# Eight-batch attention feeding a gated expert layer on one core: load order, staged keys for the second batch, and column halves of the second weight

## The chip, the cores and the metric

The kernel runs on one core of a Trainium2 chip. The metric is the time of one execution on the device in microseconds (us). The kernel before took 373.83 us as the median of three runs (373.21 to 375.34). One more execution was taken by the hardware profiler: it took 373.17 us, of which 371.5 us lie between its first and its last instruction (the span).

## The reference: what is computed

There are T = 8 batches of S = 576 tokens, H = 8 heads, D = 64 numbers per head. First comes attention with a bias that depends on the distance of two tokens alone:

```
scores = q @ k.T / sqrt(64) + bias[head, bucket(|i - j|)]     # per batch and head
x      = softmax(scores) @ v                                  # [4608 tokens, 512]
h      = x @ w_in                                             # [4608, 2048]
g      = h + sin(alpha * h) ** 2 / alpha
out    = g @ w_out                                            # [4608, 512], float32
```

All inputs are float32 in the device's memory. The kernel computes in 16-bit floats with sums in float32. Beyond a distance of 128 the bias is constant, so the kernel takes the constant out of the softmax and multiplies the exponentials by a table of ratios (the band, `m2`) only near the diagonal.

## The kernel before, in words

**Tiling.** The heads go in four pairs, so that two heads of 64 numbers fill 128 partitions. Of the 576 keys of a batch, four chunks of 128 are "A" units and the last 64 are "C" units (tile `kt`, in which a pair's two heads stand on the diagonal of a 128 x 128 block with zeros beside them). The last 64 queries are "B" and "X" units; for batch 0 they are put off into batch 1. A unit is a score matmul (TensorE, line 601), an exponential (ScalarE, line 887, 1024 columns at a time) and a product with the band (VectorE, lines 919, 932, 897; for C units line 905, on GpSimd or VectorE). Then the attention matmuls with the values follow, and after a division (lines 1137 and 1138) the result is turned into the token buffer `xT`, by TensorE (line 1209) or by a transposing DMA (line 1200). In `mh` stand copies of those parts of the band that the C and X units need (line 763); they are made from `m2` in two halves, one for each 64 partitions.

**The expert layer** works on nine blocks of 512 tokens. For each of 16 slices `f` of the 2048 middle columns there are four matmuls of 512 columns, a sine (line 1253), a square (1260 or 1262) and a sum (1267) that gives `g[f]`. The sums of TensorE stand in eight banks: six for scores and for the middle columns, two (6 and 7) for attention and for the output. `plan_mo` makes the output: for each 128 tokens 16 matmuls of 512 columns, a copy (lines 672 or 674) and a DMA. These output matmuls are the filler: TensorE does them when nothing else is ready. `xT` is a ring of 1728 tokens (three batches). A block of 512 that crosses its end, as blocks 3 and 6 do, is computed with two matmuls in place of each one.

**The order of the work** is made when the kernel is built. `Plan.run` walks through a list of tasks with estimated durations and puts each on the engine on which it can start first; the priorities only break ties within 0.02 us. `HEAD_PRI` holds priorities for tasks by their number in the list. While scores are computed, fillers are counted: at most 32 matmuls in batch 1 (`QUOTA1`), 44 in the later ones, spread evenly; past that number a filler is taken only where TensorE would else stand idle for over 0.2 us (`FILL_GAP`). What comes out is one fixed order for each engine, with semaphores between them.

**The head.** Keys and queries come from memory with a token per row and must be turned, so that the 64 numbers of a head lie along partitions. For batch 0 and batch 1, `load_nat` (line 576) loads them as they are and TensorE turns them (`plan_tr`, line 691: 12 small matmuls for a pair's keys or queries), after which ScalarE or VectorE copies them to `kT` and `qT`, and GpSimd or VectorE copies the last 64 keys into `kt` (line 716). From batch 2 on, GpSimd's DMA queue copies keys and queries, cast to 16 bits, into a buffer in the device's memory (`stage`, line 532), and SyncE's queue brings them in with a transposing DMA (lines 542 and 545). The loads on GpSimd's queue have one order, that of `plan_loads`: pairs 1 and 2 of batch 0 (`STATIC`), batch 0's values and then pair 3's keys and queries (`LOADS`), `w_in` in three parts, batch 1's keys and queries, `w_out` in four parts of four `f` each, batch 1's values, and the staging of batch 2.

Of the kernel before, what the change touches and what calls it, by code (L numbers as in the profile page):

```python
# [13 lines left out]
ALU = mybir.AluOpType  # L14
# [47 lines left out]
class Plan:  # L62
# [165 lines left out]
LOADS = ((0, (0,)), (0, (1,)), (0, (2,)), (0, (3,)), (0, (4,)), (0, (5,)), (1, (3, 0)), (1, (3, 1)))  # L228
STAGED = ()
N_WO = 4  # L230
# [186 lines left out]
def kernel(  # L417
# [21 lines left out]
    SI = 6  # L439
# [987 lines left out]
```

## Time and profile before

| what | value |
|---|---|
| median of three runs | 373.83 us (373.21 to 375.34) |
| profiled execution | 373.17 us, span 371.5 us |
| TensorE matmuls, busy | 364.9 us (98% of the span), 3661 instructions |
| ScalarE, busy | 317.6 us (86%) |
| VectorE, busy | 263.1 us (71%) |
| GpSimd, busy | 88.5 us (24%) |
| granted TensorE clock | 1.0 throughout |

In the profile PE is TensorE's matmuls, PEld its weight loads, DVE is VectorE, ACT is ScalarE, POOL is GpSimd, SP is SyncE; the ending "q" stands for the DMA queue that an engine feeds. In a row of the order in time the first two numbers are start and duration in us, then engine, line, operation, what is written and read, the shape and the count; what stands in brackets is the idle time before it and what ended that. The ends of matmuls are modelled and overlap the next one's start, so the rate of a run of matmuls is read from the distance between the starts of two rows.

### The profile page before, as it was taken

The page shows a single profiled execution, that of the slowest core. Times are in us where ns is not written, and L with a number is a line of the kernel's source. Part 1 is how long each engine was busy: PE and PEld are TensorE (multiplying, and loading weights), DVE is VectorE, ACT ScalarE, POOL GpSimd, SP SyncE. Part 2 cuts the span into 40 slices and gives each one's busy share as a digit, 9 for nine tenths or more (in the row PEclk, how much of TensorE's full clock was granted, in tenths as well). Part 3 has the DMA queues.
Part 4 walks back from the last instruction along what each step waited for, and adds up shares of the span by engine and source line. Part 5 has one row for each costly group of instructions (what it writes and reads, how often), then busy time and mean ns, then how long its engine had stood idle before and what let it go on. Part 6 is the DMA issues. An engine that isn't in the chain of part 4 may idle for free.

```text
span 371.5 us, 9081 instructions
## 1 busy us (share of the span) xinstructions
PE 364.9 (98%) x3661; PEld 199.5 (54%) x3661; DVE 263.1 (71%) x575; ACT 317.6 (86%) x434; POOL 88.5 (24%) x115
## 2 busy tenths in 40 slices
PE   8989999999999999999999999999999999999996
PEld 5655445644464445784554456444666455444443
DVE  6897876777676967696759866887769675979100
ACT  3899999999997999899989999899989997999111
POOL 8764600064000900064004600290006000000000
PEclk9999999999999999999999999999999999999999
DMA  9999991799625992399829992699259121000112
GB/s 151 164 208 206 166 151 41 124 96 126 117 52 114 104 172 77 83 135 145 116 58 148 130 146 58 136 94 178 75 89 119 64 58 48 9 29 3 71 70 85
DMA packets 147993, 39.16 MB, mean 105 GB/s; under 512 B 136416, under 2 KB 142960, under 8 KB 147952
## 3 DMA queue, kind: packets, MB, share of 16 engines
q0 software_dynamic: 99664, 18.06, 60.9%
q1 hardware_dynamic: 47920, 20.11, 22.6%
q8 instruction: 28, 0.46, 0.5%
q10 hardware_dynamic: 368, 0.43, 0.4%
q14 instruction: 13, 0.11, 0.1%
HBM read 36.84 MB, written 16.52 MB: 144 GB/s over the span
## 4 chain that ended last, share of the span: by engine, by line
PE 95%; ACT 2%; DVE 2%; issue 0%; ACTq 0%
PE pb L601 92%; ACT u L887 2%; PE pb L691 1%; DVE u L919 1%; PE pb L1209 1%; PE pb L685 0%; DVE m L674 0%; DVE mh L763 0%; DVE qT L674 0%; DVE kT L674 0%; DVE kt L716 0%; DVE zz L639 0%; ACT outs L672 0%; DVE inv_a L831 0%; DVE alphaT L825 0%
## 5 line engine op out<-in xcount | busy, mean ns | idle before, releaser
L887 ACT ACTIVATE u<-pb 128x1024 f16<-128x1024 f32 (+1 forms) x146 | 137.1, 1018 | 9.9 <-PE pb L601 8.9
L601 PE MATMUL pb<-w_out,g 128*128 128x512 f16 (+2 forms) x592 | 140.0, 374 | 0.0
L601 PE MATMUL pb<-xT,w_in 128*128 128x512 f16 (+4 forms) x704 | 127.5, 340 | 0.0
L1267 DVE SCALAR_TENSOR_TENSOR g<-sq,inv_a,pb 128x512 f16<-128x512 f16 x144 | 101.0, 743 | 6.8 <-ACT sq L1260 3.3
L1253 ACT ACTIVATE s<-pb,alphaT 128x512 f16<-128x512 f32 x144 | 93.3, 690 | 11.9 <-PE pb L601 10.8
L601 PEld LDWEIGHTS <-w_in 128*128 128x128 f16 x704 | 64.6, 98 | 57.0
L601 PEld LDWEIGHTS <-g 128*128 128x128 f16 x592 | 53.5, 98 | 63.3 <-issue 9.7
L919 DVE TENSOR_TENSOR u<-u,m 128x768 f16<-128x768 f16 (+1 forms) x128 | 61.5, 489 | 30.2 <-ACT u L887 29.7
L601 PEld LDWEIGHTS <-u 128*128 128x128 f16 x1152 | 44.6, 97 | 9.4 <-issue 1.1
L554 POOL COPY kt<-kT 64x256 f16<-64x256 f16 x12 | 5.3, 445 | 178.2 <-PE pb L601 91.6
L601 PE MATMUL pb<-v,u 128*128 128x65 f16 x1024 | 44.0, 193 | 0.2
L601 PE MATMUL pb<-qT,kT 64*128 64x64 f16 (+1 forms) x512 | 42.1, 288 | 1.6 <-ACT u L887 1.4
L1260 ACT ACTIVATE sq<-s 128x512 f16<-128x512 f16 x69 | 42.8, 637 | 1.0 <-DVE g L1267 0.3
L1262 DVE TENSOR_TENSOR sq<-s 128x512 f16<-128x512 f16 x75 | 31.0, 425 | 13.8 <-ACT s L1253 13.0
L1138 DVE TENSOR_TENSOR xn<-pb,rd 128x256 f16<-128x256 f32 (+2 forms) x59 | 28.5, 483 | 2.0
L558 POOL DMA_DIRECT2D v<-in_v_dram x32 | 28.4, 898 | 1.1 <-DMA nat<-in_k_dram 0.8
L601 PE MATMUL pb<-vh,u 128*128 128x130 f16 x128 | 28.1, 219 | 0.0
L601 PEld LDWEIGHTS <-kT 64*128 64x128 f16 x512 | 16.3, 94 | 21.4 <-issue 14.3
L672 ACT ACTIVATE outs<-pb 128x512 f32<-128x512 f32 (+2 forms) x11 | 6.2, 568 | 20.4 <-PE pb L601 20.4
L1137 DVE RECIPROCAL rd<-pb 128x4 f32<-128x4 f32 (+2 forms) x59 | 11.0, 186 | 17.6 <-PE pb L601 17.5
L674 DVE COPY outs<-pb 128x512 f32<-128x512 f32 x26 | 17.9, 690 | 4.8 <-PE pb L601 4.6
L1332 ACT ACT_TABLE_LOAD x15 | 19.2, 1283 | 0.3
(72 smaller groups left out, 189.5 us busy)
## 6 DMA issues: line engine op xcount, KB each, us to landing
out_dram<-outs SPq DMA_DIRECT2D x35, 256.0 KB, 2.2
v<-in_v_dram POOLq DMA_DIRECT2D x32, 128.0 KB, 4.8
staged_k<-in_k_dram POOLq DMA_DIRECT2D x6, 576.0 KB, 8.9
staged_q<-in_q_dram POOLq DMA_DIRECT2D x6, 576.0 KB, 11.9
w_out<-in_moe_w_out_dram POOLq DMA_DIRECT2D x4, 512.0 KB, 18.2
w_in<-in_moe_w_in_dram POOLq DMA_DIRECT2D x2, 512.0 KB, 8.5
w_in<-in_moe_w_in_dram POOLq DMA_DIRECT2D x1, 1024.0 KB, 11.1
xT<-xn SPq DMA_TRANSPOSE x47, 2.4
```

Source lines behind the costliest of these rows:

```text
L558: nc.gpsimd.dma_start(out=vs[t % 2][:, c, :, 0:D], in_=vp[128 * c : 128 * c + 128],)
L601: nc.tensor.matmul(out=out, lhsT=lhsT, rhs=rhs, start=start, stop=stop)
L674: k_of(e).tensor_copy(out=o, in_=i)
L887: nc.scalar.activation(out=o, in_=x, func=AF.Exp, scale=0.125)
L919: nc.vector.tensor_tensor(out=io, in0=io, in1=m2[:, 2 * p : 2 * p + 2, x0 : x0 + hi - lo], op=ALU.mult)
L1137: nc.vector.reciprocal(out=r, in_=x[:, :, :, D])
L1138: nc.vector.tensor_tensor(out=xn[:, 0:n].rearrange("p c (z d) -> p c z d", z=2), in0=x[:, :, :, 0:D], in1=r.unsqueeze(3).to_broadcast([128 ...
L1253: nc.scalar.activation(out=s16.v, in_=h.v, func=AF.Sin, scale=alphaT[:, f : f + 1])
L1260: nc.scalar.activation(out=sq.v, in_=s16.v, func=AF.Square)
L1262: k_of(e).tensor_tensor(out=sq.v, in0=s16.v, in1=s16.v, op=ALU.mult)
L1267: nc.vector.scalar_tensor_tensor(out=gcell[b].v[:, f, :], in0=sq.v, scalar=inv_a[:, f : f + 1], in1=h.v, op0=ALU.mult, op1=ALU.add,)
L1332: nc.scalar.preload_act_table_set(name)
```

## The change

1. Pair 3's keys and queries of batch 0 move ahead of batch 0's values in GpSimd's load order.
2. Batch 1's keys are staged in the device's memory and turned by a DMA on SyncE's queue, as those of later batches are. Its queries are still turned by TensorE. The tile that took both is now half as large.
3. `w_out` is loaded in column halves (two parts of eight `f` for each half), the first half ahead of batch 1's values and the second behind them. Block 0's output is made in eight parts of 256 columns, the first two interleaved (12 `f` of the one, 12 of the other, then the remaining four of each).
4. `xT` is a ring of 2560 tokens (five blocks). No block of 512 crosses its end; the rows of batch 4 cross it, and are written in two pieces.
5. Batch 0's C units take the band directly from `m2`, with two products of 64 partitions each in place of one with `mh`. The two copies into `mh` get a late priority.
6. Some durations in the planner are new, and `HEAD_PRI` is another table.

```
-LOADS = ((0, (0,)), (0, (1,)), (0, (2,)), (0, (3,)), (0, (4,)), (0, (5,)), (1, (3, 0)), (1, (3, 1)))
-STAGED = ()
-N_WO = 4
+LOADS = ((1, (3, 0)), (1, (3, 1)), (0, (0,)), (0, (1,)), (0, (2,)), (0, (3,)), (0, (4,)), (0, (5,)))
+STAGED = (0,)
+N_WO = 2
...
-    XN = 3 * S
+    XN = 2560
...
-    def load_w_out16(fh):
+    def load_w_out16(c, fh):
         src = moe_w_out.rearrange("(f p) n -> p f n", p=128)
+        x = slice(c * DM // 2, (c + 1) * DM // 2)
         nc.gpsimd.dma_start(
-            out=w_out16[:, 4 * fh : 4 * fh + 4, :], in_=src[:, 4 * fh : 4 * fh + 4, :]
+            out=w_out16[:, 8 * fh : 8 * fh + 8, x], in_=src[:, 8 * fh : 8 * fh + 8, x]
         )
...
-            bands["h%d" % z] = plan.add({"POOL": 0.95, "DVE": 0.37}, half, [bands[0], bands[1]], -1000 + z)
+            bands["h%d" % z] = plan.add({"POOL": 0.95, "DVE": 0.37}, half, [bands[0], bands[1]], 10012 + z)
...
             def bd(e):
+                if t == 0:
+                    for z in range(2):
+                        r = slice(64 * z, 64 * z + 64)
+                        io = u.v[r, y, 8, 384:512]
+                        k_of(e).tensor_tensor(
+                            out=io, in0=io, in1=m2[r, 2 * p + z, 64 * z : 64 * z + 128], op=ALU.mult
+                        )
+                    return
...
-            d = plan.add({"POOL": 0.6} if t == 0 and p else {"DVE": 0.25 if two else 0.15}, bd, [x] + band,
+            d = plan.add({"DVE": 0.25} if t else {"POOL": 0.8, "DVE": 0.28}, bd, [x] + band,
                          base + 10, use=[ub])
...
-        x0 = S * t % XN + q0
+        x0 = (S * t + q0) % XN
         two = parts[-1][0] > p0
+        n0 = min(nq, (XN - x0) // 128)
+        cut = [(0, nq, x0)] if two or n0 == nq else [(0, n0, x0), (n0, nq, 0)]
...
-    def plan_mo(b, a):
+    def plan_mo(b, parts, cut=0):
 
-        for c0, c1 in ((0, 384), (384, DM)) if (b, a) == (T, 3) else ((0, DM),):
...
+        parts = [(a, c0, c1, Buf("mo"), Cell()) for a, c0, c1 in parts]
+        for f, (a, c0, c1, mb, m) in [(f, x) for lo, hi in ((0, cut), (cut, NF)) for x in parts for f in range(lo, hi)]:
...
-                        z = [plan.add({"DVE": 0.35}, lambda e: load_kt(1, nc.vector), y, 10080)]
+                        z = [plan.add({"POOL": 1.1, "DVE": 0.7}, lambda e: load_kt(1, k_of(e)), y, 10080)]
...
         for b in [t] if t < T - 1 else [t, t + 1]:
+            if b == 0:
+                n = DM // 2
+                plan_mo(b, [(0, 0, n), (1, 0, n)], 12)
+                for a, c0 in ((2, 0), (3, 0), (0, n), (1, n), (2, n), (3, n)):
+                    plan_mo(b, [(a, c0, c0 + n)])
+                continue
             for a in range(4):
-                plan_mo(b, a)
+                for c0, c1 in ((0, 384), (384, DM)) if (b, a) == (T, 3) else ((0, DM),):
+                    plan_mo(b, [(a, c0, c1)])
```

More of the change, by code (lines that the diff above doesn't have):

```diff
@@ L498 @@
     nat2x = tp.tile([128, NF * DM], F16, name="nat2", tag="g", bufs=2)
-    nat2 = nat2x[0:SN, 0 : 2 * H * SI * D].rearrange("s (kq h x) -> s kq h x", kq=2, h=H)
+    nat2 = nat2x[0:SN, 0 : H * SI * D].rearrange("s (h x) -> s h x", h=H)
     nat1x = sgl.tile([128, 2 * (H - 2) * SI * D], F16, name="nat1")
@@ L658, in load_nat2 @@
     def load_nat2(kq):
-        load_nat(nat2[:, kq], 0, H, (k, q)[kq][1], P_)
+        load_nat(nat2, 0, H, (k, q)[kq][1], P_)
     uts = nat1x.rearrange("p (b h k q) -> p b h k q", b=2, h=NP, k=9)
@@ L692, in mm @@
                         out=c.v[64 * z : 64 * z + 64, x : x + SN],
-                        in_=(nat1 if t == 0 else nat2)[:, kq, h, D * i : D * i + D],
+                        in_=(nat2[:, h] if t else nat1[:, kq, h])[:, D * i : D * i + D],
                         identity=id_sb[0:SN, 0:SN],
@@ L718, in tail @@
                 )
-        return [x], [plan.add({"POOL": 0.5, "DVE": 0.24}, tail, [x], pri + 30)]
+        return [x], [plan.add({"POOL": 0.95, "DVE": 0.48}, tail, [x], pri + 30)]
     def plan_table():
@@ L796, in plan_loads @@
             if kq in STAGED:
-                pool("kq%d" % kq, (2.3, 2.6)[kq], lambda kq=kq: stage(1, kq), (4.4, 5.0)[kq])
+                pool("kq%d" % kq, (2.3, 2.6)[kq], lambda kq=kq: stage(1, kq), (4.2, 4.4)[kq])
             else:
@@ L805, in plan_loads @@
         for f in range(4):
-            wq.append(("wo%d" % f, 0.76, lambda f=f: load_w_out16(f), 2.65))
+            wq.append(("wo%d" % f, 0.76, lambda f=f: load_w_out16(f // 2, f % 2), 2.65))
         n = N_WO
@@ L813, in plan_loads @@
             if kq in STAGED:
-                loads["t%d" % kq] = load("SP", 2.8, lambda kq=kq: (load_kT, load_qT)[kq](1), 2.6, 9030 + kq,
+                loads["t%d" % kq] = load("SP", 2.8, lambda kq=kq: (load_kT, load_qT)[kq](1), 3.1, 9030 + kq,
                                          [loads["kq%d" % kq][1]], [loads["t0"][0]] if "t0" in loads else [])
@@ L891, in plan_unit @@
         band = [] if t or kind in "BX" else [bands[x] for x in (
-            ("h0", "h1") if kind == "C" else ((1, 2), (0, 1, 2), (0, 1, 2), (0, 1))[c])]
+            (0, 1) if kind == "C" else ((1, 2), (0, 1, 2), (0, 1, 2), (0, 1))[c])]
+        if t < 2 and kind == "X" or t == 1 and kind == "C":
+            band = [bands["h0"], bands["h1"]]
         if kind == "X":
@@ L897, in bd @@
                 nc.vector.tensor_tensor(out=io, in0=io, in1=mh[:, :, 128:192], op=ALU.mult)
-            done["X"] = plan.add({"DVE": 0.25}, bd, [x], base + 10, use=[ub])
+            done["X"] = plan.add({"DVE": 0.25}, bd, [x] + band, base + 10, use=[ub])
         elif kind == "C":
@@ L1102, in plan_tail @@
         x = plan.add({"DVE": 0.67}, norm, [mark], base, new=[xb], use=[ab])
-        x0 = S * t % XN + 512
+        x0 = (S * t + 512) % XN
         if t:
@@ L1197, in turn @@
             def turn(e):
-                o = (xT[:, p0 : p0 + 2, x0 : x0 + 128] if two else
-                     xT[:, p0, x0 : x0 + 128 * nq].rearrange("d (c q) -> d c q", c=nq))
-                nc.sync.dma_start_transpose(
-                    out=o, in_=xn.v[:, 0:nq].rearrange("p c d -> p (c d)"))
+                for a, b, c in cut:
+                    o = (xT[:, p0 : p0 + 2, c : c + 128] if two else
+                         xT[:, p0, c : c + 128 * (b - a)].rearrange("d (c q) -> d c q", c=b - a))
+                    nc.sync.dma_start_transpose(
+                        out=o, in_=xn.v[:, a:b].rearrange("p c d -> p (c d)"))
             made(plan.add({"SP": 0.3}, turn, [x], base, use=[xb]))
@@ L1215, in put @@
         def put(e):
-            o, i = xT[:, p0, x0 : x0 + 128 * nq], tr_.v[:, 0 : 128 * nq]
             if two:
-                o, i = xT[:, p0 : p0 + 2, x0 : x0 + 128], i.rearrange("p (y q) -> p y q", y=2)
-            copy_on(e, o, i)
+                copy_on(e, xT[:, p0 : p0 + 2, x0 : x0 + 128],
+                        tr_.v[:, 0:256].rearrange("p (y q) -> p y q", y=2))
+                return
+            for a, b, c in cut:
+                copy_on(e, xT[:, p0, c : c + 128 * (b - a)], tr_.v[:, 128 * a : 128 * b])
         n = 128 * nq
@@ L1298, with mm, cp @@
     mo_last = []
-    def plan_mo(b, a):
-        for c0, c1 in ((0, 384), (384, DM)) if (b, a) == (T, 3) else ((0, DM),):
-            mb, ob, m = Buf("mo"), Buf("outs"), Cell()
-            n = c1 - c0
-            for f in range(NF):
-                def mm(e, f=f, m=m, mb=mb, c0=c0, c1=c1):
-                    if f == 0:
-                        m.v = bank(mb)
-                    full(
-                        m.v[:, 0 : c1 - c0], gcell[b].v[:, f, 128 * a : 128 * a + 128],
-                        w_out16[:, f, c0:c1], f == 0, f == NF - 1,
-                    )
-                mo_last[:] = [plan.add({"PE": t_pe(n)}, mm, mo_last[:] + [gdone[(b, f)]] + ([loads["wo%d" % (f // 4)][1]] if b == 0 else []),
-                                       500000000 + 4 * b + a,
-                                       new=[mb] if f == 0 else [],
-                                       use=[gbuf[b]] if f == 0 else [gbuf[b], mb])]
-                mo_last[0].fill = True
-            def cp(e, m=m, c0=c0, c1=c1):
+    def plan_mo(b, parts, cut=0):
+        parts = [(a, c0, c1, Buf("mo"), Cell()) for a, c0, c1 in parts]
+        for f, (a, c0, c1, mb, m) in [(f, x) for lo, hi in ((0, cut), (cut, NF)) for x in parts for f in range(lo, hi)]:
+            def mm(e, f=f, a=a, c0=c0, c1=c1, mb=mb, m=m):
+                if f == 0:
+                    m.v = bank(mb)
+                full(
+                    m.v[:, 0 : c1 - c0], gcell[b].v[:, f, 128 * a : 128 * a + 128],
+                    w_out16[:, f, c0:c1], f == 0, f == NF - 1,
+                )
+            mo_last[:] = [plan.add({"PE": t_pe(c1 - c0)}, mm, mo_last[:] + [gdone[(b, f)]] + ([loads["wo%d" % (2 * c0 // DM * 2 + f // 8)][1]] if b == 0 else []),
+                                   500000000 + 4 * b + (a if b else a / 2 + 4 * c0 / DM),
+                                   new=[mb] if f == 0 else [],
+                                   use=[gbuf[b]] if f == 0 else [gbuf[b], mb])]
+            mo_last[0].fill = True
+            if f < NF - 1:
+                continue
+            def cp(e, a=a, c0=c0, c1=c1, m=m):
                 o = new_outs()[:, 0 : c1 - c0]
@@ L1325, in cp @@
                 nc.sync.dma_start(out=out[r0 : r0 + 128, c0:c1], in_=o)
+            n = c1 - c0
             y = plan.add({"DVE": t_dve(n), "ACT": t_act(n)}, cp, mo_last[:], CP_PRI,
-                         new=[ob], use=[mb])
+                         new=[Buf("outs")], use=[mb])
             y.s_only = True
@@ L1391 @@
         for b in [t] if t < T - 1 else [t, t + 1]:
+            if b == 0:
[3 more added lines that the diff above has]
+                    plan_mo(b, [(a, c0, c0 + n)])
+                continue
             for a in range(4):
-                plan_mo(b, a)
+                for c0, c1 in ((0, 384), (384, DM)) if (b, a) == (T, 3) else ((0, DM),):
+                    plan_mo(b, [(a, c0, c1)])
     for i, x in HEAD_PRI.items():
```

284 rows, old and new, of the table HEAD_PRI are left out of this document.

## The prediction

> **What bounds the kernel now.** I read the page first, then the chain of waits in order of time, then busy times by stretches, then the order of work of single engines and the landings of single loads.
>
> ```profile
> span 371.5 us, 9081 instructions
> PE 364.9 (98%) x3661; PEld 199.5 (54%) x3661; DVE 263.1 (71%) x575; ACT 317.6 (86%) x434; POOL 88.5 (24%) x115
> PE 95%; ACT 2%; DVE 2%; issue 0%; ACTq 0%
> 29.60:66.00 36.40, 36.40 (x397) 18.36 (x393) 27.30 (x60) 34.34 (x49) 9.15 (x14) 1.00 1.25 136
> 66.00:72.00 6.00, 5.60 (x118) 4.17 (x115) 5.11 (x16) 5.98 (x8) 0.00 (x0) 1.00 0.79 114
> ```
>
> The page's busy times and its chain that ended last both lie on TensorE. The last two rows are stretches: start and end, length, busy time of PE, PEld, DVE, ACT and POOL, clock, DMA share, GB/s. From 29.6 us, where block 0 of the expert layer begins, to 66 us TensorE has no idle time, and ScalarE has 36.40 - 34.34 = 2.06 us: the two are nearly level. Whether that busy time is real work is read from the starts of matmul rows:
>
> ```profile
> 59.38 2.33 PE L601 MATMUL pb<-w_out,g 128*128 128x512 f16 x10
> 61.64 0.82 PE L601 MATMUL pb<-qT,kT 64*128 64x512 f16 x6
> 311.63 7.93 PE L601 MATMUL pb<-xT,w_in 128*128 128x512 f16 x36
> 319.40 0.22 PE L601 MATMUL pb<-vh,u 128*128 128x130 f16 x1
> ```
>
> 36 matmuls take 319.40 - 311.63 = 7.77 us, 0.216 each. Ten take 61.64 - 59.38 = 2.26, which is 0.10 more than ten times 0.216: the price of changing from whole-array matmuls to scores of 64 rows. So a TensorE task taken out here shortens the kernel by its spacing, as long as ScalarE and VectorE follow, and a gap costs its length. Ahead of 29.6 us three engines share the limit:
>
> ```profile
> 14.78 8.41 ACT L887 ACTIVATE u<-pb 128x1024 f16<-128x1024 f32 x10
> 23.39 5.18 ACT L887 ACTIVATE u<-pb 128x1024 f16<-128x1024 f32 x6 [0.20 <-PE pb L601]
> 31.32 0.38 ACT L672 ACTIVATE xT<-pb 128x256 f16<-128x256 f16 x1 [0.33 <-PE pb L1209]
> 32.18 1.84 ACT L1253 ACTIVATE s<-pb,alphaT 128x512 f16<-128x512 f32 x3 [0.48 <-PE pb L601]
> ```
>
> ScalarE's exponentials run from 14.78 to 28.57 with 0.20 idle, and it then waits 0.33 + 0.48 = 0.81 for TensorE ahead of the sines. VectorE's part is in the chain of waits:
>
> ```profile
> 15.12 0.86 DVE mh L763
> ...
> 19.20 0.67 DVE qT L674
> ...
> 20.34 0.67 DVE kT L674
> ...
> 21.53 1.84 PE pb L601 x38
> ```
>
> The copy into mh, and two copies for pair 3, stand on VectorE ahead of the band products for which TensorE waits until 21.5, when it gets on with the value matmuls.
>
> **The change part by part.**
>
> *Keys of batch 1.* The chain holds the turning of batch 1's eight groups, 96 small matmuls:
>
> ```profile
> 33.44 0.63 PE pb L691 x24
> 35.90 0.38 PE pb L691 x12
> 37.25 0.63 PE pb L691 x24
> 39.71 0.63 PE pb L691 x24
> 46.49 0.38 PE pb L691 x12
> ```
>
> That is 2.65 us. Four groups stay: 4 x 0.38 = 1.52 if each goes alone, 2 x 0.63 = 1.26 in pairs. I take the middle: a gain of **1.26** (ends 1.13 and 1.39). The copies to kT and kt of these groups go too; the former stood on ScalarE:
>
> ```profile
> 36.32 0.65 ACT L672 ACTIVATE kT<-pb 128x576 f16<-128x576 f16 x1
> 51.98 6.93 SPq L1325 DMA_DIRECT2D out_dram<-outs  x2
> ```
>
> Four times 0.65 = 2.6 us of ScalarE: the engine that is nearly level is relieved by twice what TensorE is, and does not hold the gain back. The transposing DMA that is added goes on SyncE's queue, whose first row after 29 us is the one at 51.98, so nothing there is behind it. The two new copies to kt fall into GpSimd's idle time (9.15 busy of 36.40); without that cover they would be VectorE's, which has 9.1 us free.
>
> *What the staging does to the loads behind it.* These are GpSimd's queue and the landings:
>
> ```profile
> 16.45 0.80 POOL L576 DMA_DIRECT2D nat<-in_k_dram  x1
> 18.75 1.57 POOL L585 DMA_DIRECT2D w_out<-in_moe_w_out_dram  x2
> 42.44 2.21 POOL L532 DMA_DIRECT2D staged_k<-in_k_dram  x1 [0.25 <-issue]
> ```
>
> ```profile
> w_out<-in_moe_w_out_dram POOLq DMA_DIRECT2D x4, 512.0 KB, 18.2
> staged_k<-in_k_dram POOLq DMA_DIRECT2D x1, 576.0 KB, 8.6
> kT<-staged_k SPq DMA_TRANSPOSE x1, 6.2
> ```
>
> ```profile
> 46.80 2.12 PE L601 MATMUL pb<-w_out,g 128*128 128x512 f16 x9
> ```
>
> The second part of w_out is issued at 18.75 + 0.79 = 19.5 and lands at 19.5 + 18.2 = 37.7, the first matmul with w_out is at 46.80. The issue of a staging takes 2.21 us of GpSimd in place of 0.8 for the plain load, and the loads of w_out and of batch 1's values stand behind it. On the DMA engines the lower end of the delay is nothing (the same bytes are read), the upper one is the staging's whole landing and the transposing DMA's, 8.6 + 6.2 = 14.8. Nearest is that only the transposing DMA is new traffic: 6.2, so the first half of w_out is complete at 43.9. With the gains of this sum TensorE comes to w_out at about 46.80 - 1.26 - 0.65 = 44.9, and to f = 8, which needs the second load, eight matmuls of 0.108 later, at 45.8. It costs **nothing**, with 1.9 us to spare; that margin is the slower rival below. The second half of w_out, behind the values, is asked for only after 64 half matmuls (6.9 us of work spread among scores).
>
> *Column halves.* 64 matmuls of 512 columns become 128 of 256. What a matmul costs beyond its columns is in the chain, where block 3 is cut at the ring's end and block 4 is not:
>
> ```profile
> 152.21 39.54 PE pb L601 x443
> 191.92 39.38 PE pb L601 x379
> ```
>
> 64 matmuls more for 0.16 us: **+0.16** for the halves. The eight copies and output DMAs in place of four lie on VectorE, which is busy for 27.30 of 36.40 us.
>
> What each new matmul brings besides is a weight load:
>
> ```profile
> L601 PEld LDWEIGHTS <-g 128*128 128x128 f16 x592 | 53.5, 98 | 63.3 <-issue 9.7
> ```
>
> With its 98 ns in the open, 64 x 0.098 = 6.3 us would be added. The two rows above speak against it (0.16 us for 64 more matmuls with their loads), and so does the spacing of 0.216, in which 512 columns leave no room for 98 ns.
> The Trainium skill, "TensorE: Matmul & The Clock Gate", section "The mechanism", says that weight loads overlap matmuls in flight only where their row groups differ. All rows are used here, so by that rule the loads would stand in the open and the sum would come out 6.3 us higher; the trace does not agree.
>
> *The ring of 2560.* Blocks 3 and 6 are no longer cut: 2 x 0.16 = a gain of **0.32**. Batch 4's rows are written in two pieces, which adds three DMAs on SyncE's queue and a copy; output matmuls cover it, else it is one 0.38 us copy (the row at 31.32).
>
> *Bands for the C units.* The mh copy of 0.86 leaves VectorE's list ahead of the first value matmuls. In its place come two products per pair:
>
> ```profile
> 18.27 0.52 POOL L905 TENSOR_TENSOR u<-u,mh 128x128 f16<-128x128 f16 x1 [0.25 <-issue]
> 20.12 0.21 DVE L905 TENSOR_TENSOR u<-u,mh 128x128 f16<-128x128 f16 x1
> ```
>
> If VectorE keeps the one pair that it has, two halves at 0.21 add 0.21: a gain of 0.86 - 0.21 = **0.65**. The worst end is all eight on VectorE, 8 x 0.21 - 0.21 = 1.47 against 0.86, a loss of 0.6. The best is bounded by ScalarE, which can give up its idle 0.20 + 0.81 = 1.0. mh is made later, for the late units of batch 0, in time that VectorE or GpSimd has.
>
> *Pair 3 ahead of the values.* The eight loads are only permuted, so their last one lands when it did:
>
> ```profile
> 11.04 0.69 POOL L576 DMA_DIRECT2D nat<-in_q_dram  x1
> ```
>
> ```profile
> nat<-in_q_dram POOLq DMA_DIRECT2D x1, 144.0 KB, 5.7
> ```
>
> That is 16.7 us, now for the values, and the first value matmuls wait until 21.5: **0**, hidden behind the band products. If that cover shrinks by the 0.65 above, 4 us are left.
>
> *Grain of the filler.* The limit of 32 filler matmuls in batch 1's scores stays, but each is half as long. Past it a filler is taken only for gaps over 0.2 us, so each of the nine runs of scores may leave up to 0.2 idle, 1.8 in all. The lower end is a gain of 0.40, the one gap of that stage now:
>
> ```profile
> 68.83 0.41 PE L601 MATMUL pb<-qT,kT 64*128 64x64 f16 x16 [0.40 <-ACT u L887]
> ```
>
> Short matmuls fit small gaps better, and most of the stage has no gap, so I stay near the present state: **+0.2**. The new table of priorities redraws the order elsewhere; each change of kind more or less is 0.10, and I put it at 0 with three pairs either way, 0.6.
>
> **The sum.** -1.26 + 0.16 - 0.32 - 0.65 + 0.2 = -1.87. The profiled execution took 373.17 us (371.5 and 1.67 around it), so 371.3 for one like it. It lies 0.66 below the median of the runs and 0.04 below the fastest; against the median the forecast is 373.83 - 1.87 = 372.0.
>
> **The rivals.**
>
> *More in the head.* Pair 3's turned keys and queries come earlier, so VectorE's two copies of 0.67 may fall into its gaps before 15 us, and the value matmuls begin up to 1.3 us sooner still. ScalarE's 1.0 caps it: -1.26 + 0.16 - 0.32 - 1.0 + 0.2 = -2.2, 371.6. For it speaks that both copies are in the chain; against it, that VectorE has other work then.
>
> *The turning was cover.* If ScalarE and VectorE set the pace of block 0, its 1.26 us only become a wait for banks: -1.87 + 1.26 = -0.6, 373.2. For it: 34.34 of 36.40 busy. Against it: ScalarE loses 2.6 us of copies.
>
> *Fine filler, open gaps.* The full 1.8: -1.87 + 1.6 = -0.3, 373.5. It holds too if the redrawn order does not do what the parts say. Against it: fillers past the limit still take every long gap.
>
> *w_out too late (slower).* TensorE's order is fixed, so a wait at f = 8 holds batch 0's late scores and batch 1's first scores, and with them ScalarE's exponentials. From 45.8 us on each us of delay costs one; the change is a loss past 45.8 + 1.9 = 47.7. Landing at 50, between my 43.9 and the bound 37.7 + 14.8 = 52.5, costs 4.2: 376.1. For it: a saturated queue in which w_out takes 18.2 us to land. Against it: the plain load that is replaced was as many bytes.
>
> *Weight loads in the open:* -1.87 + 6.3 = +4.4, 378.2.
>
> **How the numbers follow.** The forecast has 0.40, more in the head 0.22, the cover 0.11, open gaps 0.11, late w_out 0.14, weight loads 0.02. About 0.5% (1.87 us) is what can be told from no change here, and the forecast lies on that edge: half of it counts as faster. Faster 0.20 + 0.22 = 0.42; same 0.20 + 0.22 = 0.42; slower 0.16. The favourable ends add to -1.39 + 0.16 - 0.32 - 1.0 - 0.4 - 0.6 = -3.6 (370.2), the unfavourable without a late load to -1.13 + 0.16 - 0.32 + 0.6 + 1.8 = +1.1; I let the upper end stop at 374.4, which leaves out the late load and little else.
>
> **What would show it.** Four turning groups of batch 1 in place of eight, and no kT copies on ScalarE between 33 and 41 us. No mh copy between 15 and 16, and value matmuls from about 20.9. The matmuls of blocks 3 and 6 at 379 in a piece of 39.38. TensorE's idle time from 45 to 72 us below 0.6. I am wrong if TensorE waits for w_out near 45, if block 0 starts no earlier than 29.6, or if the periods of the later batches change by more than the ring's 0.16.

## The result and the profile after

| | before | after |
|---|---|---|
| median of the runs | 374.81 us (22 runs, 372.25 to 375.75) | 372.48 us (22 runs, 371.18 to 374.97) |
| ratio | | 0.9948, 95% interval 0.9929 to 0.9968 |
| profiled execution | 373.17 us, span 371.5 | 371.38 us, span 369.5 |

The change made the kernel faster by 0.5%; the forecast was 372.0. The medians fell by 2.33 us, the profiled pair by 1.79, where 1.87 was forecast. The page of the kernel after, and below it its chain of waits in order of time (start, length, what):

```profile
span 369.5 us, 8853 instructions
PE 360.7 (98%) x3545; PEld 193.5 (52%) x3545; DVE 263.3 (71%) x579; ACT 315.9 (85%) x433; POOL 91.0 (25%) x111
PE 92%; DVE 3%; DMA 1%; ACT 1%; POOL 1%; issue 0%; DVEq 0%; ACTq 0%; POOLq 0%
```

```profile
35.82 0.63 PE pb L692 x24
...
37.42 0.38 PE pb L692 x12
...
43.08 0.38 PE pb L692 x12
...
110.44 0.17 PE pb L1223 x3
...
150.16 39.38 PE pb L602 x380
...
268.81 39.38 PE pb L602 x379
308.19 0.17 PE pb L1223 x3
308.36 57.62 PE pb L602 x330
...
366.05 0.28 ACT outs L673
```

TensorE still sets the time. The turning of batch 1 has gone from 96 small matmuls to 48 (0.63 + 0.38 + 0.38 = 1.39 us, from 2.65), and the pieces of blocks 3 and 6 have lost the 0.16 each that the ring's end cost.

To see where the gain lies I cut the execution at four points of TensorE and ScalarE: the first w_in matmul (block 0), the first turned result of batch 2, that of batch 7, and the last copy of an output. For the kernel after the first is the second row here, of TensorE's order; the others are in the chain above.

```profile
18.22 0.23 PE L602 MATMUL pb<-vh,u 128*128 128x130 f16 x1
28.52 1.46 PE L602 MATMUL pb<-xT,w_in 128*128 128x512 f16 x6
```

| stretch of the profiled execution, us | before | after | difference |
|---|---|---|---|
| start to block 0 (the head) | 29.60 | 28.52 | -1.08 |
| block 0 to batch 2 | 82.90 | 81.92 | -0.98 |
| batch 2 to batch 7 | 198.06 | 197.75 | -0.31 |
| batch 7 to the last copy | 57.86 | 57.86 | 0 |
| last copy to the span's end | 3.08 | 3.45 | +0.37 |
| around the span | 1.67 | 1.88 | +0.21 |
| sum | 373.17 | 371.38 | -1.79 |

From block 0 to the last copy ("the body") 338.82 us became 337.53: -1.29. The body hardly depends on the execution: three kernels below that leave it alone (e5, e6, e12) have 338.82 again. The head does depend on it, and it is where the prediction missed something. In the tables below "block 0 at" and "body", in us, are of the one profiled execution of each kernel, and the first of the two says little by itself; the medians and ratios are over all runs.

### The profile page after: what moved, and what is told of

It is laid out like the page before. It is cut to its first block, busy times and chain, and to the rows that moved or that the text cites. A ratio compares the mean times of both kernels' runs of the same rounds, so it can differ in the third digit from the quotient of the medians.

```text
span 369.5 us, 8853 instructions
## 1 busy us (share of the span) xinstructions
PE 360.7 (98%) x3545; PEld 193.5 (52%) x3545; DVE 263.3 (71%) x579; ACT 315.9 (85%) x433; POOL 91.0 (25%) x111
## 4 chain that ended last, share of the span: by engine, by line
PE 92%; DVE 3%; DMA 1%; ACT 1%; POOL 1%; issue 0%; DVEq 0%; ACTq 0%; POOLq 0%
PE pb L602 90%; DVE u L930 2%; DMA nat<-in_k_dram 1%; ACT u L888 1%; POOL nat L576 1%; PE pb L1223 1%; PE pb L692 0%; DVE xn L1149 0%; DVE qT L675 0%; DVE m L675 0%; POOL tabN L617 0%; DVE rd L1148 0%; POOL id_sb L619 0%; DVE xT L675 0%; ACT outs L673 0%
## 5 line engine op out<-in xcount | busy, mean ns | idle before, releaser
L602 PE MATMUL pb<-w_out,g 128*128 128x512 f16 (+3 forms) x656 | 140.6, 354 | 0.0
L602 PE MATMUL pb<-xT,w_in 128*128 128x512 f16 x576 | 127.1, 380 | 0.0
L602 PEld LDWEIGHTS <-g 128*128 128x128 f16 x656 | 59.8, 98 | 59.8 <-issue 9.2
L602 PEld LDWEIGHTS <-w_in 128*128 128x128 f16 x576 | 55.7, 98 | 65.3 <-DVE xT L675 0.3
L930 DVE TENSOR_TENSOR u<-u,m 128x512 f16<-128x512 f16 (+1 forms) x128 | 62.7, 497 | 31.0 <-ACT u L888 30.6
L1276 ACT ACTIVATE sq<-s 128x512 f16<-128x512 f16 x68 | 41.8, 628 | 1.0 <-DVE g L1283 0.3
L1149 DVE TENSOR_TENSOR xn<-pb,rd 128x256 f16<-128x256 f32 (+2 forms) x59 | 28.5, 483 | 2.0
L673 ACT ACTIVATE outs<-pb 128x512 f32<-128x512 f32 (+3 forms) x11 | 6.0, 541 | 20.6 <-PE pb L602 20.6
L675 DVE COPY outs<-pb 128x512 f32<-128x512 f32 (+1 forms) x30 | 18.7, 628 | 5.4 <-PE pb L602 5.1
```

What stands on the lines that cost most here:

```text
L602: nc.tensor.matmul(out=out, lhsT=lhsT, rhs=rhs, start=start, stop=stop)
L675: k_of(e).tensor_copy(out=o, in_=i)
L930: nc.vector.tensor_tensor(out=io, in0=io, in1=m2[:, 2 * p : 2 * p + 2, x0 : x0 + hi - lo], op=ALU.mult)
L1149: nc.vector.tensor_tensor(out=xn[:, 0:n].rearrange("p c (z d) -> p c z d", z=2), in0=x[:, :, :, 0:D], in1=r.unsqueeze(3).to_broadcast([128 ...
L1276: nc.scalar.activation(out=sq.v, in_=s16.v, func=AF.Square)
```

## The experiments

Two kinds of kernel are used. In the first, one part of the change is put into the kernel before and the planner draws a new order; the old priorities go along with their tasks. In the second the order of the kernel before (every task, its engine and its banks) is written into the kernel, and only the edit moves:

```
     def run(self, t0):
+        for i, e, ks in ORDER:          # the recorded order
+            ...
+            t.emit(ENG[e])
+
+    def run_planned(self, t0):
         free = dict(t0)
```

### One part alone, order drawn anew

```
e1  -    XN = 3 * S
    +    XN = 2560                       # and the rows written in two pieces
e2  -STAGED = ()
    +STAGED = (0,)                       # and nat2 at half its size, kt on POOL or DVE
e3   LOADS with pair 3 first; C units take the band from m2; mh late
e4  -N_WO = 4
    +N_WO = 2                            # and load_w_out16(c, fh), plan_mo in halves
```

> The kernel before with the ring of 2560 tokens alone. Theory 'each part pays its own TensorE work': the pieces of the chain for blocks 3 and 6 fall from 39.54 us with 443 matmuls to 39.38 with 379, 0.32 us in all, and nothing else moves; block 0's first matmul with w_in stays at 29.6 us. Theory 'the clock': the order of the head is the one of before, so if the head's gain of 1.08 us was the earlier full clock, this kernel shows the first matmul with w_in near 28.5 whenever its small turning matmuls (12 in 0.69 us at the slow clock, 0.45 at the full one) are fast by 7 us, and near 29.6 whenever they are slow until 12 us.

> The kernel before with batch 1's keys staged and turned by a DMA, nothing else. Theory 'own work': four turning groups fewer, so the stretch from block 0's first matmul with w_in to its last shrinks by 1.1 to 1.4 us (before: 29.60 to the turning group at 46.42, 16.8 us), and the whole by the same. Rival 'the turning was cover': that stretch shrinks by less than 0.4 us, and TensorE shows idle time there. Rival 'w_out late': TensorE waits for w_out near 45 us.

> The kernel before with pair 3's loads ahead of the values and with the C units' band taken from m2, nothing else. Theory 'VectorE's list': the first value matmul comes at 18 to 19 us in place of 21.1 and block 0 starts 0.65 to 1.1 us earlier, 28.5 to 28.9, whatever the clock does before 13 us. Theory 'the clock': block 0 starts near 29.6 if the turning matmuls are slow until 12 us and near 28.5 only if they are fast by 7 us. Beyond block 0's start no change.

> The kernel before with w_out and block 0's output in column halves, nothing else. Theory 'own work': 64 matmuls more cost 0.14 to 0.16 us, block 0 starts as before, and batch 2's first turned result (112.5 us before) comes 0.1 to 0.2 later. Theory 'grain': the limit of 32 fillers leaves gaps among batch 1's scores, and TensorE's idle time from 45 to 72 us rises from 0.4 to over 1 us, with the marker 0.6 to 1.8 us later. By the rule that weight loads stand in the open it would be 6.3 us later.

| part alone | median, us | ratio to before (374.53), 95% | block 0 at | body |
|---|---|---|---|---|
| e1 ring | 373.93 | 0.9993 (0.9967 to 1.0019) | 31.07 | 338.50 |
| e2 keys staged | 375.05 | 1.0026 (1.0001 to 1.0051) | 29.85 | 339.78 |
| e3 loads and bands | 376.32 | 1.0072 (1.0047 to 1.0096) | 30.18 | 341.40 |
| e4 halves | 377.26 | 1.0078 (1.0048 to 1.0108) | 30.77 | 341.29 |

The ring alone gives what was forecast: 0.31 from batch 2 to batch 7. Its block 0 fits neither theory, as 31.07 is later than both said. The other three are slower than nothing (e2 only just), though together they are faster. For e2 TensorE's order names the waits, and its stretch from 45 to 72 us their sum (27.00 - 25.67 = 1.33 idle, where the kernel before has 0.40):

```profile
48.52 0.41 PE L600 MATMUL pb<-qT,kT 64*128 64x64 f16 x16 [0.68 <-DVE g L1266]
51.27 0.39 PE L600 MATMUL pb<-qT,kT 64*128 64x512 f16 x2 [0.52 <-ACT nat L886]
```

```profile
45.00:72.00 27.00, 25.67 (x328) 13.82 (x327) 19.55 (x48) 25.98 (x32) 5.95 (x5) 1.00 1.53 123
```

In e4 the last piece of the chain has grown from 57.62 us with 330 steps to

```profile
310.92 61.07 PE pb L601 x346
```

16 output matmuls of 512 columns are left for the end: 16 x 0.216 = 3.46, as the piece has grown by 3.45. Batch 2, which is rid of them, comes only 1.04 us sooner after block 0 (81.86, from 82.90); where the other 2.4 went was not followed. The 2.58 us that e3 loses lie between block 0 and batch 2 too, and its waits were not followed either. So these kernels do not price the parts. What they price besides is a planner with a table made for another list of tasks; the next kernels part the two.

### One part alone, order kept

```
e5   load order: -v0 v1 v2 v3 v4 v5 k3 q3     +k3 q3 v0 v1 v2 v3 v4 v5
e6   e5, and the C units' bands from m2, the two mh copies on POOL behind v3 of batch 1
e7   batch 1's keys staged and turned by DMA; their eight
     turning matmul groups and copies taken out of the order
e8   the kernel after in its own order; all four w_out loads ahead of batch 1's values
```

> The instruction order of before kept fixed on every engine, with one change: on GpSimd's queue pair 3's keys and queries go ahead of batch 0's values. Theory 'wait and clock': in the ring kernel TensorE stood 2.20 us for pair 3's keys at 14.4 to 16.6 us, its granted clock then fell to 0.5 from 18 to 24 us, and block 0 began at 31.07; with the loads ahead that wait is gone, so no clock of 0.5 shows between 15 and 26 us, block 0 begins at 28.5 to 29.6, and the group of runs near 375.4 us (13 of the first 22 of before) is gone: median 372.3 to 373.3. Rival 'hidden' (the prediction's 0 for this part): the times spread as those of before do, with a group near 375.4.

> As the kernel with the loads moved in a fixed order, and besides the C units of batch 0 take the band from m2, with the two mh copies on GpSimd behind batch 1's values. Theory 'VectorE's list': block 0 begins another 0.5 to 0.9 us earlier than with the loads alone at the same clock. Rival: no change, under 0.2 us, because ScalarE's exponentials set the pace by then.

> The instruction order of before kept fixed, with batch 1's four key groups of turning matmuls, their copies to kT and to kt left out, and the staging, one transposing DMA and two copies to kt put in. Theory 'own work': from block 0's first matmul with w_in to its last it takes 15.4 to 15.7 us (16.8 before), and batch 2's first turned result comes 1.1 to 1.3 us earlier counted from block 0's start (82.9 us before). Rival 'keys late': the transposing DMA lands near 50 us as in the staged kernel with its own order (49.9), TensorE waits for it near 50 us, and of the 1.3 less than 0.6 is left at batch 2.

> The instruction order of after kept fixed, with one change: all four parts of w_out stand ahead of batch 1's values on GpSimd's queue. Theory 'keys late': the transposing DMA of the staged keys, which lands 13.4 us after its issue in after and 19.0 in the staged kernel, lands at 47 to 50 us in place of 43.9; the first scores of batch 1 (48.65 us in after) wait for it, and the whole is 0.5 to 2 us longer. Rival 'no share': the landing stays within 1 us of 43.9 and the time within 0.3 us of after's.

| edit | median, us | ratio to before (374.06), 95% | block 0 at | body |
|---|---|---|---|---|
| e5 loads | 373.28 | 0.9965 (0.9944 to 0.9986) | 30.45 | 338.82 |
| e6 loads and bands | 372.15 | 0.9939 (0.9913 to 0.9966) | 27.35 | 338.82 |
| e7 keys staged | 373.21 | 0.9983 (0.9961 to 1.0005) | 30.96 | 337.35 |
| e8 after, w_out ahead | 372.43 | 0.9962 (0.9935 to 0.9989) | 29.98 | 337.52 |

With the order kept each edit has a lower median than the kernel before. The keys are worth 338.82 - 337.35 = 1.47 us of the body. With the order drawn anew the bodies were 339.78 for the same keys (e2) and 341.40 for the same loads and bands (e3), so the new order alone cost 2.43 and 2.58 us: it is the order that made these parts look slow. In e7 the turned keys land near 49, as the rival "keys late" said, but TensorE's idle time from 45 to 72 us is 0.40 as before. And e5, two loads moved and nothing else, is faster by 0.35%, for which the prediction had nothing; with the bands (e6) the head alone gives as much as the whole change did. What the loads are worth is seen in e1, whose head has the order of the kernel before:

```profile
16.58 0.45 PE L691 MATMUL pb<-id_sb,nat 96*64 96x96 f16 x12 [2.20 <-DMA nat<-in_k_dram]
```

TensorE stands 2.20 us for pair 3's keys (1.48 in e2, 2.31 in e4, 2.52 in e7, which have the same load order). In the profile of before that wait isn't there:

```profile
11.78 0.69 PE L691 MATMUL pb<-id_sb,nat 96*64 96x96 f16 x12
16.44 0.45 PE L691 MATMUL pb<-id_sb,nat 96*64 96x96 f16 x12
```

In that execution TensorE ran its first small matmuls slowly until 12.8 us (a group of 12 turnings took 0.69, against 0.45 in e1) and came to the keys when they had landed. In e1 a second thing follows. Its stretches (start and end, length, TensorE busy, granted clock, DMA share, GB/s):

```profile
14.00:16.00 2.00, 0.38 (x4) 1.00 1.29 159
16.00:18.00 2.00, 1.42 (x28) 0.97 1.17 190
18.00:20.00 2.00, 1.56 (x10) 0.50 1.24 202
20.00:22.00 2.00, 1.80 (x14) 0.50 1.16 217
22.00:24.00 2.00, 2.00 (x33) 0.50 1.13 209
```

After the idle stretch the granted clock falls to 0.50 for some 6 us, and block 0 starts at 31.07 instead of 29.60. Each run lists its mean granted clock. Over 81 runs of the kernel before, those beside e1 to e12, these means lie near four values, and the time goes with them; in the kernel after it does not do so in order:

| mean granted clock | before: runs, median us | after: runs, median us |
|---|---|---|
| 0.998 to 1.0 | 21, 373.20 | 13, 371.50 |
| about 0.995 | 9, 373.39 | 4, 373.88 |
| about 0.991 | 23, 374.34 | 4, 373.14 |
| about 0.986 | 28, 375.24 | 1, 373.52 |

60 of 81 executions of the kernel before lose clock, 9 of 22 of the kernel after. By these medians the change is worth 1.70 us between executions that keep the clock; the medians over all runs differ by 2.33, since it also loses the clock less often. A start like that of the profile of before, slow at a printed clock of 1.00, is among the first group, so it is still a mixture: 18 of the 21 runs of before lie at 373.16 to 373.65, as the profiled one does, and 3 at 371.61 to 372.01. The fastest of these is only 0.43 us behind the fastest run of the kernel after (371.18), though the body alone is worth 1.29; no profile of such a run was taken, so what its head did stays open. The steps are 0.0047 of the span apart: half the clock for 2 x 0.0047 x 371.5 = 3.5 us each, an estimate. The Trainium skill, "TensorE: Matmul & The Clock Gate", section "Part 1: The HAM clock gate", states a window of about 3.4 us that runs freely, and half the clock after an idle one. The length and the half agree with these rows; that a whole window must be idle does not, as no wait in e1's head is longer than 2.20 us. A window whose start has nothing to do with the kernel's would also explain why one kernel falls in some executions and not in others; no run here shows the window itself.

The profiles of e5 and e7 still have such a fall (0.50 at 20 to 24 us and at 18 to 24), so e5 does not remove it for good, against what was expected of it, and its block 0 at 30.45 is later than the 28.5 to 29.6 expected. The group of runs near 375.4 us is gone, as expected: the slowest of its 12 took 374.06. The profile of e6 has none, which is why its block 0 at 27.35 and e5's at 30.45 cannot be set against each other to price the bands. The fastest runs of e6 and e5, 370.92 and 371.33, differ by 0.41.

In e8 the copies that wait for the turned keys run at 46.34, 2.3 us later than in the kernel after, and the body is 337.52 against 337.53: the order of loads behind the keys costs nothing there. The keys came later than the rival said, and the time was not the longer one of the theory.

### The halves, the waits and the clock

A dummy is a matmul on zeros (`zz`) whose result nothing reads; the kernel before has a few such already.

```
e9   before's order: loads, bands, staged keys and the ring; no halves
e10  e9, and ahead of the scores g=1, i=1, 2, 3:
+    full(pb[:, 6, 0:512], zz[:, 0:128], zz[:, 0:512], True, True)    # x2, x2, x1
e11  the kernel after in its own order, the same dummies x4, x1, x3 in its three waits
e12  the kernel before in its own order, x6 ahead of pair 3's turning, then as e10
```

> The instruction order of the kernel before, kept as it was, with three parts of the change put into it: pair 3's keys and queries ahead of the values, the bands copied late from the table, batch 1's keys staged and turned by DMA; and the turned results' ring of 2560 columns. The output stays in whole columns, w_out in quarters, and the planner draws nothing anew. If the parts add up as they did one at a time (-1.48 for the keys, -0.31 for the ring), the time from the first w_in matmul to the last copy of the output is 338.82 - 1.48 - 0.31 = 337.03 us, 0.5 less than in the whole change (337.53): that 0.5 is then what the column halves and the order drawn anew for them cost. If the halves are what makes the keys' staging pay (the rival), it is 337.5 or more, with TensorE waiting near 44 to 50 us for the keys. Block 0 starts near 27.4 without a fall of the granted clock in the head and near 28.5 to 29 with one; median 371 to 371.8, faster than the whole change by 0.7 to 1.5 us.

> The kernel without halves with five dummy matmuls of 512 columns added where TensorE waits for ScalarE's exponentials between 16 and 19 us (two, two and one, into a bank that nothing else uses then). If it is TensorE's idleness there that makes the granted clock fall to 0.5 near 18 us, the profile shows no fall, block 0 starts as early as without the dummies and without a fall (27.4, at most 0.2 later), and the runs of the group lie closer together, the median lower by 0.3 to 0.7 us. If the fall comes from something else, the times and their spread are those of the kernel without dummies, or up to 0.5 us longer.

> The changed kernel, in its own order, with eight dummy matmuls of 512 columns in the three waits of TensorE between 16 and 21.2 us (four, one and three; 1.07, 0.33 and 1.02 us in its profile). If idleness makes the clock fall, no fall in the profile, block 0 at 28.5 to 28.8, and a median of 371.2 to 371.7 where the changed kernel had 372.48. If not, a median of 372.3 or more.

> The kernel before, in its own order, with six dummy matmuls of 512 columns in the wait for pair 3's keys (2.20 us where the head ran at full clock) and five in the waits for the exponentials after it; nothing else is changed. This parts the wait from the fall of the clock. If the fall costs most of it, the wait stays and the clock doesn't fall: block 0 at 29.4 to 30.0 rather than 30.8 to 31.1, median 373.0 to 373.4, against 374.1 for the kernel before. If the wait itself costs it, block 0 stays at 30.7 or later and the median within 0.3 us of the kernel before.

| kernel | median, us (range, runs) | ratio to before (374.35), 95% | block 0 at | body |
|---|---|---|---|---|
| e9 no halves | 371.31 (370.87 to 372.84, 8) | 0.9931 (0.9907 to 0.9956) | 30.36 | 337.21 |
| e10 and dummies | 371.26 (370.32 to 372.24, 6) | 0.9920 (0.9893 to 0.9948) | 27.33 | 338.04 |
| e11 after, dummies | 371.35 (370.71 to 372.00, 6) | 0.9925 (0.9899 to 0.9951) | 28.93 | 337.53 |
| e12 before, dummies | 373.74 (372.47 to 375.46, 12) | 0.9984 (0.9964 to 1.0005) | 30.48 | 338.82 |

*Halves.* Without them the body of e9 is 337.21, 0.32 shorter than that of the kernel after (337.53). That is what the halves and the order drawn for them cost; 0.18 less than the sum of the parts had promised (337.03 for e9), and e9 lies between the forecasts of its theory and its rival. What they buy shows in e10, whose profiled execution brought block 0 3 us earlier than e9's (in that of e9 the first matmuls ran slowly, as in the one of before):

```profile
47.38 1.46 PE L620 MATMUL pb<-w_out,g 128*128 128x512 f16 x6 [0.76 <-DMA w_out<-in_moe_w_out_dram]
```

```profile
48.87 0.85 POOL L573 COPY kt<-kT 64x256 f16<-64x256 f16 x2 [8.20 <-DMA kT<-staged_k]
```

TensorE waits 0.76 us for a part of w_out, and the turned keys land only at 48.87, when the first scores of batch 1 start (48.86). The body is longer than e9's by 0.83, and TensorE's idle time from 45 to 72 us is 1.19, from 0.40: the wait for w_out is nearly all of it. So with the head early a load holds TensorE up, and the time is that of the rival (that the keys' staging needs the halves), though in e9 it is not; but the wait is for w_out, and none for the keys shows. In the kernel after, with half the columns of w_out asked for first, nothing waits there:

```profile
44.26 2.24 PE L602 MATMUL pb<-w_out,g 128*128 128x256 f16 x19
```

```profile
44.01 0.84 POOL L554 COPY kt<-kT 64x256 f16<-64x256 f16 x2 [1.78 <-DMA kT<-staged_k]
```

Its keys land 4.9 us earlier than e10's.

*The clock.* With dummies in the waits no execution of e10 or e11 lies below 0.998 (6 of 6 each, against 5 of 8 of e9 and 13 of 22 of the kernel after), and 10 of 12 of e12 lie at or above it, against 21 of 81 of the kernel before. The clearest pair is the last, where nothing but the dummies is changed: filling TensorE's idle time in the head keeps the clock up in most executions. Idle time does not always bring it down, though. The kernel after had 2.52 of 6 us idle in its profile (e1 2.64 from 14 to 20 us), at a clock of 1.00:

```profile
16.00:18.00 2.00, 0.93 (x9) 1.00 1.26 203
18.00:20.00 2.00, 1.58 (x24) 1.00 1.24 213
20.00:22.00 2.00, 0.97 (x14) 1.00 1.14 214
```

In the median the dummies bring e10 nothing over e9, though, where 0.3 to 0.7 was expected. The stretches of e11, to be set beside those of e1 and of the kernel after:

```profile
14.00:16.00 2.00, 1.79 (x31) 1.00 2.05 152
16.00:18.00 2.00, 1.90 (x18) 1.00 1.30 197
18.00:20.00 2.00, 1.96 (x26) 1.00 1.25 213
20.00:22.00 2.00, 1.61 (x15) 1.00 1.14 211
```

The median of e11 is in the range expected of it, its block 0 at 28.93 a little late. All six runs of e11 are at or under 372.00 us; of the 22 of the kernel after 14 are above that. The intervals of the ratios overlap, though (0.9899 to 0.9951 and 0.9929 to 0.9968), and so do those of e9 and e10 with the kernel after: no version is shown to be faster than it; three lie 1.1 to 1.2 us lower in their medians, beside a kernel before that was 0.46 lower too. e12 decides less than it was meant to: it shows that the dummies keep the clock, and not what the wait and the fall cost. Its median fits neither of its two forecasts, and its interval holds no change. Its profiled execution, the slowest of the 12, doesn't say why: there the clock was near 0.50 from 8 to 14 us, before any of the added dummies, and these then held back the turning of pair 3, which needed no wait for its keys by then.

## Why the prediction was right, point by point

**Keys of batch 1: right, a little small.** Forecast -1.26. The rows of the turning fall from 2.65 to 1.39, exactly that; the whole edit gave -1.47 in the body (e7; in the median 0.9983 of before, with an interval that reaches 1.0005). The 0.21 beyond lies in the matmuls around and wasn't followed further.

**Ring: right.** Forecast -0.32, measured -0.31 (e1 and the kernel after).

**Halves +0.16 and grain +0.2: their sum right.** e9 against the kernel after gives 0.32 for both, with the order drawn anew. They weren't parted. TensorE's idle time from 45 to 72 us was forecast below 0.6 and is 27.00 - 26.78 = 0.22, from 0.40: the fine filler opened no gaps, so that rival falls.

```profile
45.00:72.00 27.00, 26.78 (x410) 19.80 (x409) 19.19 (x52) 24.83 (x30) 4.21 (x2) 1.00 1.34 135
```

The body was thus forecast at -1.26 + 0.16 - 0.32 + 0.2 = -1.22, and measured at -1.29. No weight load of the 64 added matmuls stood in the open, which would have been 6.3 us.

**Pair 3 ahead of the values, "0, hidden": this step failed.** It was read from the one profiled execution, in which a slow start hid the wait. In the four others with this load order and a quick start (e1, e2, e4, e7) the wait is 1.48 to 2.52 us, and the clock is near 0.5 after it; the two loads alone are worth 0.35% (0.14 to 0.56%). That the profiled pair differs by 1.79, so near the forecast 1.87, is in part luck: the head's -1.08 sets a slow start without that wait (before) against a quick start with waits of its own (after), and neither is what the sum's -0.65 and 0 stood for. It is also nearer to the -1.0 of the rival "more in the head". That rival's sign was borne out by the first value matmul, at 18.22 and not 20.9 (from 21.14 before; the 21.5 of the prediction is a later row). VectorE's last copy of keys or queries now starts at 16.37, where the kernel before had pair 3's two at 19.12 and 20.26. But TensorE waits for that copy:

```profile
17.17 0.60 PE L602 MATMUL pb<-qT,kT 64*128 64x512 f16 x4 [1.07 <-DVE qT L675]
```

The rival's cap was reasoned from ScalarE, and it missed the wait for pair 3's keys and the clock as well.

**Bands -0.65: not priced.** e6 is lower than e5 by 1.13 us in the median, with intervals that overlap, and the clock in the two profiles differs.

**Staging's delay: cost nothing, for a wrong size.** The transposing DMA was put at 6.2 us; it landed 13.4 us after its issue in the kernel after, 18.2 in e7, e9 and e10. The row of the kernel after:

```profile
kT<-staged_k SPq DMA_TRANSPOSE x1, 13.4
```

The late w_out of the slower rival is a real wait, but of e10: 0.76 us with w_out in whole columns and the head early. With the halves that the change brings along it did not come.

**The turning was cover: refuted.** Taking the turning out gave all of its time and more in the body (e7).

**Not foreseen:** 0.37 us more after the last copy and 0.21 more around the span, in one execution each.

Two of the rivals' times are a rounding off: 371.96 + 4.2 = 376.2 and 371.96 + 6.3 = 378.3. No chance hangs on that.

## What to carry to other kernels

A profile is one execution. Before a wait is costed at nothing because it isn't there, ask whether the engine was late by chance, and look at when the data land against when the engine could have come. Price a part of a planned kernel with the order held fixed, since a planner that redraws with an old table can lose more than the part is worth (2.43 us against 1.47 for the keys). Idle time of TensorE in the head can cost the granted clock besides its length: 21 of 81 runs of the kernel before kept it, and 10 of 12 with dummy matmuls in the waits. How the loss divides between the wait and the clock was not shown.

## What the runs showed of the hardware

The granted clock fell to 0.50 after TensorE had been busy for 0.38 of 2 us, with a single wait of 2.20 us, and the mean clocks of 81 executions lie in steps that come to about 3.5 us at half clock each, an estimate (1.0, 0.995, 0.991, 0.986), the last 2.0 us slower than the first by the median. Idle time alone does not decide it: with TensorE busy for 0.93, 1.58 and 0.97 of three stretches of 2 us the clock stayed at 1.00 in the kernel after. A head whose first matmuls were slow until 12.8 us can print a granted clock of 1.00 throughout all the same (the kernel before: 0.69 for a group that takes 0.45). A transposing DMA of 576 KB took 6.2 us to land in the kernel before and 13.4 to 19.0 (after, e2) beside the loads of w_out and of batch 1's values on GpSimd's queue.
